# Cached-key attention block: the value loads move from SP's DMA queue to GpSimd's

## The chip, the cores and the metric

The kernel runs on one core of a Trainium2 chip. The metric is the device time of one execution in microseconds; a shorter time is better. The median of three runs is compared.

## What is computed

For a batch of 8, 112 query rows and a model width of 640, there are 32 heads of width 192 and a cache of 512 keys and values per batch and head. All inputs are bf16.

```python
q = (x @ wq).reshape(8, 112, 32, 192).transpose(0, 2, 1, 3)
scores = einsum("bhqd,bhkd->bhqk", q, k_cache) * 192 ** -0.5
p = softmax(scores, axis=-1)
o = einsum("bhqk,bhkd->bhqd", p, v_cache)
out = o.transpose(0, 2, 1, 3).reshape(8, 112, 32 * 192) @ wo
```

The keys and the values are 50 MB each and are read once. The weights `wq` and `wo` are 7.9 MB each.

## The kernel before

Work is cut into **pairs** of heads. The 32 heads form four stages (`hg`, 0 to 3) of eight heads; within a stage the loop runs over the eight batches, and within a batch over four pairs (`lp`), so there are 128 pairs, numbered `ip`. Two pairs that follow each other share one **group** `g` (64 groups): one load of keys and one load of values covers four heads.

All engines follow the same list of periods. In period `i` TensorE (PE) executes, in this order: the scores S of pair `i` (L166 to L169, which read the key tile), half of the transposes of the softmax weights of pair `i-1` (L182), the product with the values PV of pair `i-2` (L200, L206), the other half of the transposes, the output projection O of pair `i-3` (L234, L235), and the query projection Q of pair `i+2` (L262). ScalarE (ACT) does the exponentials and part of the PSUM evictions, VectorE (DVE) the row maxima, scalings and the rest. The order is written out by hand in `DEFAULT_ORDERS`, and semaphores join the engines: `sS` counts scores done, `sPV` counts value products done, `mK[j]`, `mV[j]`, `mWQ`, `mWO` and `mXN` are raised by 16 when a load has landed.

**Keys.** SP issues one transposing DMA for each group (`issue_k`, L477) into one of six buffers `kt[g % 6]`, after the scores of group `g-6` are done. The source is cut into rows of 256 bytes, 3,072 of them in a load of 768 KB.

**Values.** SP issues one plain DMA for each group (`issue_v`, L489), directly after the group's keys, into one of six buffers `vt[g % 6]`, after the value products of group `g-6` are done. A load is 128 partitions by 4 heads by 768 elements: 512 rows of 1,536 bytes, 768 KB. The last two value buffers hold `x` at the start, so value loads 4 and 5 also wait until PE has transposed `x` (`sXT`).

SP's list is thus K0, V0, K1, V1 and so on, with three waits at the start: K1 waits for weight block 1 of stage 0, K2 for block 3, K3 for the last part of `x`.

**Weights.** GpSimd (POOL) issues them, with `x`, in a list ordered by period (`dmas`, filled by `add`). Stage 0 is loaded at the start: four blocks of `wq` (L578, 480 KB) and four of `wo` (L599, L603, L605), the latter after the landing of certain keys. The weights of stages 1 to 3 are cut into 20 pieces of `wq` (L581, 96 KB) and 16 of `wo` (L601 to L607), and spread over the stage before. Each of these pieces waits in `k_landed_wait` until the keys and the values of a certain group have landed:

```python
gK = min(NGRP - 1, max(0, (period + cfg.get("KOFF", 2)) // 2))
W(gp, mK[gK % NKB], 16 * (gK // NKB + 1))
gV = min(NGRP - 1, max(0, (period + cfg.get("VOFF", 0)) // 2))
if period >= 2:
    W(gp, mV[gV % NVB], 16 * (gV // NVB + 1))
```

GpSimd executes its list in order, so what stands behind a wait waits too.

At the start PE transposes batch 0 of `x` (L402), projects pairs 0 and 1 with weight blocks 0 and 1, computes the scores of pair 0, projects pair 2 with block 2, transposes the other seven batches of `x`, and goes on with period 1.

Of the kernel before, what the change touches and what calls it, by code (L numbers as in the profile page):

```python
# [20 lines left out]
def build_mha_kernel(nc, x, k_cache, v_cache, wq, wo, out, cfg=None):  # L21
    cfg = dict(cfg or {})
# [12 lines left out]
    G = 4  # L35
# [8 lines left out]
    def heads_of(ip):  # L44
        u, hg, b, lp = unit_of(ip)
        h0 = hg * HG + 2 * lp
        return b, h0
# [22 lines left out]
    with ExitStack() as es:  # L70
# [55 lines left out]
        def wsem(lst, hg, lp):  # L126
            return lst[(hg % 2) * PPU + lp]
# [18 lines left out]
        def W(eng, s, v):  # L146
            if v > 0:
                eng.wait_ge(s, v)
# [312 lines left out]
        @block.sync  # L461
        def _(sp):
            if not XPE:
                sp.dma_start_transpose(xT_sb[:, :, :], x.rearrange("b s d -> (b s) d")).then_inc(mX, 16)
            EARLY_LEAD = cfg.get("EARLY_LEAD", 0)
            EARLY_N = cfg.get("EARLY_N", 12)

            def issue_k(g):
                b, h0 = heads_of(2 * g)
                kb = g % NKB  # L470
                if g >= NKB:
                    W(sp, sS, 4 * (g - NKB) + 4)
                if EARLY_LEAD and g < EARLY_N and g >= EARLY_LEAD:
                    W(sp, sS, 4 * (g - EARLY_LEAD) + 4)
                src = k_cache[b, h0:h0 + G].rearrange("u (r q) d -> (u r) (q d)", q=4)
                dst = kt[kb][:].rearrange("p a m c -> p (a m) c")
                sp.dma_start_transpose(dst, src).then_inc(mK[kb], 16)  # L477

            def issue_v(g):
                b, h0 = heads_of(2 * g)  # L480
                vb = g % NVB
                if g >= NVB:
                    W(sp, sPV, 2 * (g - NVB) + 2)
                if EARLY_LEAD and g < EARLY_N and g >= EARLY_LEAD + 1:
                    W(sp, sPV, 2 * (g - EARLY_LEAD - 1) + 2)
                if XPE and g in (NVB - 2, NVB - 1):
                    W(sp, sXT, B)
                src = v_cache[b, h0:h0 + G].rearrange("u (r q) d -> r u (q d)", q=4)
                sp.dma_start(vt[vb][:, :, :], src).then_inc(mV[vb], 16)  # L489

            STARTUP = cfg.get("STARTUP", False) and PPU == 4 and NGRP > 5
            if STARTUP:
                issue_k(0)
                issue_k(1)
                issue_v(0)
                W(sp, wsem(mWQ, 0, 3), 16)
                issue_k(2)
                issue_v(1)
                W(sp, wsem(mWO, 0, 1), 48)
                issue_k(3)  # L500
                issue_v(2)
                W(sp, wsem(mWO, 0, 3), 48)
                issue_k(4)
                issue_v(3)
                issue_v(4)
                for g in range(5, NGRP):
                    issue_k(g)
                    issue_v(g)
            else:
                VLAG = cfg.get("VLAG", 0)  # L510
                SPGATE = cfg.get("SPGATE", True) and XPE and PPU >= 4
                for g in range(NGRP + VLAG):
                    if g < NGRP:
                        G1 = cfg.get("SPG1", 1)
                        if SPGATE and g == G1:
                            W(sp, wsem(mWQ, 0, 1), 16)
                        if SPGATE and g == G1 + 1:
                            W(sp, wsem(mWQ, 0, 3), 16)
                        if SPGATE and g == G1 + 2 and B > 4:
                            W(sp, mXN[2], 16)  # L520
                        issue_k(g)
                    if 0 <= g - VLAG < NGRP:
                        issue_v(g - VLAG)
            for b in range(B):
                u = (NHG - 1) * B + b
                if OUTT:
                    W(sp, aOF, b + 1)
                else:
                    W(sp, dOA, u + 1)
                sp.dma_start(out[b], o_out[:, b, :]).then_inc(mOUT[b % 2], 16)  # L530
            for ob in range(2):
                nb = len([b for b in range(B) if b % 2 == ob])
                if nb:
                    sp.wait_ge(mOUT[ob], 16 * nb)

        @block.gpsimd
        def _(gp):
# [11 lines left out]
            def add(need, fn):  # L549
                dmas.setdefault(need, []).append(fn)  # L550
# [4 lines left out]
            def k_landed_wait(period):  # L555
                gK = min(NGRP - 1, max(0, (period + cfg.get("KOFF", 2)) // 2))
                W(gp, mK[gK % NKB], 16 * (gK // NKB + 1))
                gV = min(NGRP - 1, max(0, (period + cfg.get("VOFF", 0)) // 2))
                if period >= 2:
                    W(gp, mV[gV % NVB], 16 * (gV // NVB + 1))  # L560

            STARTUP = cfg.get("STARTUP", False) and PPU == 4 and NGRP > 5

# [20 lines left out]
            def wo_dma(hg, lp, piece, period):  # L584
                wb = hg % 2
                if hg >= 2:
                    W(gp, sO, (hg - 1) * B * PPU)
                if hg == 0 and XPE:
                    if piece == 0:
                        gK = min(NGRP - 1, max(0, period // 2 + cfg.get("WOG", -2)))  # L590
                        W(gp, mK[gK % NKB], 16 * (gK // NKB + 1))
                elif period >= 0 and (hg == 0 or cfg.get("PACE_ALL", True)):
                    k_landed_wait(period)
                r0 = hg * WQC + lp * 2 * DH
                rows = wo[r0:r0 + 2 * DH, :].rearrange("(two r) d -> r two d", two=2, r=DH)
                dstv = wo_sb[:, wb, 3 * lp:3 * lp + 3, :]
                sm = wsem(mWO, hg, lp)
                if piece == 0 and hg == 0:
                    gp.dma_start(dstv[:, 0:3:2, :], rows[0:128, :, :]).then_inc(sm, 16)  # L599
                elif piece == 0:  # L600
                    gp.dma_start(dstv[:, 0, :], rows[0:128, 0, :]).then_inc(sm, 16)  # L601
                elif piece == 1:
                    gp.dma_start(dstv[0:64, 1, :], rows[128:192, 0, :]).then_inc(sm, 16)  # L603
                elif piece == 2:
                    gp.dma_start(dstv[64:128, 1, :], rows[128:192, 1, :]).then_inc(sm, 16)  # L605
                else:
                    gp.dma_start(dstv[:, 2, :], rows[0:128, 1, :]).then_inc(sm, 16)  # L607

            for hg in range(NHG):
                items = []  # L610
                for lp in range(PPU):
                    if wq_npieces(hg) == 1:
                        items.append((first_pair(hg, lp) - 2, 0, lp, "wq", None))
                    else:
                        for dcp in range(DC):
                            items.append((first_pair(hg, lp) - 2, 0, lp, "wq", dcp))
                    for piece in range(wo_npieces(hg)):
                        items.append((first_pair(hg, lp) + 3, 1, lp, "wo", piece))
                items.sort()
                for j, (need, _, lp, kind, piece) in enumerate(items):  # L620
                    if hg == 0:
                        period = need
                    else:
                        start = first_pair(hg - 1, 0) + cfg.get("W_START", 8)
                        span = B * PPU - cfg.get("W_START", 8) - 6
                        period = start + (j * span) // len(items)
                    if kind == "wq":
                        add(period, lambda hg=hg, lp=lp, period=period, piece=piece: wq_dma(hg, lp, period, piece))
                    else:
                        add(period, lambda hg=hg, lp=lp, piece=piece, period=period: wo_dma(hg, lp, piece, period))  # L630
            if XPE and B > 1:
                def fx():
                    n1 = min(B, 4)
                    gp.dma_start(vt[NVB - 2][0:SQ, :, :].rearrange("p u c -> p (u c)")[:, D:n1 * D].rearrange("p (b d) -> p b d", d=D),
                                 x[1:n1].rearrange("b s d -> s b d")).then_inc(mXN[1], 16)
                    if B > 4:
                        gp.dma_start(vt[NVB - 1][0:SQ, :, :].rearrange("p u c -> p (u c)")[:, 0:(B - 4) * D].rearrange("p (b d) -> p b d", d=D),
                                     x[4:B].rearrange("b s d -> s b d")).then_inc(mXN[2], 16)
                dmas.setdefault(-1, []).append(fx)
# [62 lines left out]
```

## Time and profile before

| What | Value |
|---|---|
| Median of 3 runs | 501.38 us |
| Lowest and highest run | 500.34 and 502.07 us |
| Span of the profiled execution | 499.2 us |
| Median of the runs less this span | 2.2 us |
| PE busy in the span | 479.0 us (96%) |
| VectorE busy | 446.6 us (89%) |
| ScalarE busy | 355.1 us (71%) |
| GpSimd busy | 71.5 us (14%) |
| Moved by DMA | 119.90 MB, mean 240 GB/s |
| Key loads (SP, 64), issue to landing | median 9.9 us |
| Value loads (SP, 64), issue to landing | median 5.8 us |

The page has no time of the profiled execution beside its span, which runs from its first to its last instruction; the runs are timed around the whole execution. A difference that is worked out in the span is therefore carried over to the median. In the lists of DMA queues, q1 is what SP issues and q0 is what GpSimd issues; a share counts the time of the packets against 16 engines, and as packets of one engine overlap it can be over 100%.

### The profile page before, as it was taken

How to read it: one execution, taken by the hardware profiler on the slowest of the kernel's cores; microseconds unless marked ns; L12 is line 12 of the kernel's file. 1: busy time of each engine (PE TensorE's matmuls, PEld its weight loads, DVE VectorE, ACT ScalarE, POOL GpSimd, SP SyncE). 2: the span in 40 equal slices, each digit the busy share in tenths (PEclk: the TensorE clock that was granted, in tenths of full speed). 3: DMA queues.
4: the chain of work that ended last, by engine and by line, in shares of the span. 5: the costliest groups of instructions: out<-in, count | busy, mean ns of one | idle time of the engine just before them, and what ended most of it. 6: DMA issues, size and time to landing. Idle time of an engine off the chain costs nothing.

```text
span 499.2 us, 18678 instructions
## 1 busy us (share of the span) xinstructions
PE 479.0 (96%) x6824; PEld 418.9 (84%) x6824; DVE 446.6 (89%) x1610; ACT 355.1 (71%) x898; POOL 71.5 (14%) x133
## 2 busy tenths in 40 slices
PE   1799999999999999999999999999999999999995
PEld 1788888888888888888888888888888888888884
DVE  2589999998999999999999999999999999999994
ACT  1277777777777777777777777777777777777773
POOL 7110133131000133131000122322000000000000
PEclk9999999999999999999999999999999999999999
DMA  9999999999999999999999999999999999999000
GB/s 227 305 285 239 244 256 274 249 265 292 237 249 263 281 261 259 245 265 251 239 247 236 259 290 279 240 282 260 233 272 254 255 260 255 238 258 261 3 14 25
DMA packets 239738, 119.90 MB, mean 240 GB/s; under 512 B 201840, under 2 KB 236480, under 8 KB 239648
## 3 DMA queue, kind: packets, MB, share of 16 engines
q1 hardware_dynamic: 233472, 101.82, 94.4%
q0 software_dynamic: 6176, 16.88, 11.3%
q8 instruction: 56, 0.92, 0.8%
q14 instruction: 34, 0.28, 0.2%
HBM read 67.21 MB, written 1.15 MB: 137 GB/s over the span
## 4 chain that ended last, share of the span: by engine, by line
PE 93%; DMA 2%; issue 1%; DVE 1%; POOL 1%; ACT 0%; DVEq 0%; POOLq 0%; ACTq 0%
PE ps L262 19%; PE ps L234 16%; PE ps L182 13%; PE ps L200 10%; PE ps L206 8%; PE ps L166 6%; PE ps L169 6%; PE ps L167 6%; PE ps L168 6%; PE ps L235 4%; DMA wq_sb<-in_wq_dram 2%; DVE xT_sb L409 1%; POOL wq_sb L578 0%; DVE s_sb L332 0%; DVE o_out L377 0%
## 5 line engine op out<-in xcount | busy, mean ns | idle before, releaser
L284 ACT ACTIVATE p_sb<-s_sb,nmx 112x512 bf16<-112x512 f32 x256 | 181.6, 712 | 3.1 <-DVE s_sb L332 2.1
L332 DVE TENSOR_SCALAR_CACHE_REDUCE s_sb<-ps 112x512 f32<-112x512 f32 x256 | 166.3, 686 | 16.2 <-PE ps L169 14.0
L278 ACT ACTIVATE pT_sb<-ps 128x448 bf16<-128x448 f32 x128 | 69.5, 543 | 88.4 <-PE ps L182 88.4
L262 PE MATMUL ps<-xT_sb,wq_sb 128*128 128x112 bf16 x1920 | 118.0, 215 | 5.2 <-DMA wq_sb<-in_wq_dram 5.2
L234 PE MATMUL ps<-wo_sb,oT_sb 128*112 128x512 bf16 x384 | 118.3, 380 | 0.0
L262 PEld LDWEIGHTS ps<-xT_sb,wq_sb 128*128 128x128 bf16 x1920 | 103.8, 99 | 16.7 <-DMA wq_sb<-in_wq_dram 4.4
L182 PE MATMUL ps<-dg,p_sb 112*128 112x112 bf16 x1024 | 94.0, 214 | 1.8 <-ACT p_sb L284 1.6
L272 ACT ACTIVATE qs<-ps 128x336 bf16<-128x336 f32 x128 | 57.6, 450 | 45.0 <-PE ps L262 41.8
L338 DVE CAST pT_sb<-ps 128x448 bf16<-128x448 f32 x128 | 79.9, 624 | 5.3 <-PE ps L182 1.4
L235 PE MATMUL ps<-wo_sb,oT_sb 128*112 128x128 bf16 x384 | 83.9, 219 | 0.0
L182 PEld LDWEIGHTS ps<-dg,p_sb 112*128 112x128 bf16 x1024 | 64.5, 98 | 14.4 <-ACT p_sb L284 1.9
L166 PE MATMUL ps<-kt,qs 128*112 128x256 bf16 x256 | 70.8, 277 | 2.5 <-issue 1.9
L200 PE MATMUL ps<-pT_sb,vt 128*128 128x112 bf16 x1024 | 71.8, 213 | 0.1
L167 PE MATMUL ps<-kt,qs 128*112 128x256 bf16 x256 | 70.4, 275 | 0.0
L169 PE MATMUL ps<-kt,qs 128*112 128x256 bf16 x256 | 70.4, 275 | 0.0
L168 PE MATMUL ps<-kt,qs 128*112 128x256 bf16 x256 | 70.3, 275 | 0.0
L234 PEld LDWEIGHTS ps<-wo_sb,oT_sb 128*112 128x112 bf16 x384 | 49.7, 129 | 22.3
L581 POOL DMA_DIRECT2D wq_sb<-in_wq_dram x60 | 32.1, 539 | 188.5 <-DMA kt<-in_k_cache_dram 182.4
L308 DVE TENSOR_SCALAR dg<-ident,rinv 112x112 bf16<-112x112 bf16 x256 | 52.9, 249 | 5.0 <-issue 0.5
L200 PEld LDWEIGHTS ps<-pT_sb,vt 128*128 128x128 bf16 x1024 | 56.5, 98 | 0.9 <-issue 0.5
L291 ACT ACTIVATE oT_sb<-ps 128x336 bf16<-128x336 f32 x128 | 55.3, 432 | 1.7 <-PE ps L206 1.7
L235 PEld LDWEIGHTS ps<-wo_sb,oT_sb 128*112 128x112 bf16 x384 | 50.0, 130 | 0.0
(38 smaller groups left out, 498.5 us busy)
## 6 DMA issues: line engine op xcount, KB each, us to landing
vt<-in_v_cache_dram SPq DMA_DIRECT2D x64, 768.0 KB, 5.8
wq_sb<-in_wq_dram POOLq DMA_DIRECT2D x60, 96.0 KB, 5.3
wo_sb<-in_wo_dram POOLq DMA_DIRECT2D x24, 160.0 KB, 5.6
wo_sb<-in_wo_dram POOLq DMA_DIRECT2D x32, 80.0 KB, 5.1
wq_sb<-in_wq_dram POOLq DMA_DIRECT2D x4, 480.0 KB, 10.2
wo_sb<-in_wo_dram POOLq DMA_DIRECT2D x4, 320.0 KB, 10.9
out_dram<-o_out SPq DMA_DIRECT2D x8, 140.0 KB, 4.4
kt<-in_k_cache_dram SPq DMA_TRANSPOSE x64, 9.9
```

The costliest lines, as they stand in the source:

```text
L166: pe.matmul(bk[:, 0:256], qs[:, qb, EA[h], :], ktb[:, :, 0, cs], start=True, stop=False)
L167: pe.matmul(bk[:, 0:256], qs[:, qb, ET[h], :], ktb[:, :, 1, cs], start=False, stop=True)
L168: pe.matmul(bk[:, 256:512], qs[:, qb, OC[h], :], ktb[:, :, 2, cs], start=True, stop=False)
L169: pe.matmul(bk[:, 256:512], qs[:, qb, OH[h], :], ktb[:, :, 1, cs], start=False, stop=True).then_inc(sS, 1)
L182: mm = pe.matmul(ps[:, 2 + h, j * SQ:(j + 1) * SQ], p_sb[:, pslot, j * 128:(j + 1) * 128], dg[:, dslot, :], start=True, stop=True)
L200: pe.matmul(ps[:, 4, oc * SQ:(oc + 1) * SQ], vtb[:, u, q * 192: q * 192 + 128], pT_sb[:, ptb, h, j * SQ:(j + 1) * SQ], start=(j == 0), sto ...
L234: pe.matmul(ps[0:SQ, 6, :], oT_sb[:, ob, c, :], wo_sb[:, wb, 3 * lp + c, 0:512], start=first, stop=last)
L235: mm = pe.matmul(ps[0:SQ, 7, 0:128], oT_sb[:, ob, c, :], wo_sb[:, wb, 3 * lp + c, 512:640], start=first, stop=last)
L262: mm = pe.matmul(ps[:, 5, c * SQ:(c + 1) * SQ], lhsT, xT_sb[:, dc, b * SQ:(b + 1) * SQ], start=(dc == 0), stop=(dc == DC - 1))
L284: act.activation(p_sb[:, Hh % NP, :], s_sb[:, Hh % NSS, :], ACTF.Exp, bias=nmx[:, Hh % NS:Hh % NS + 1], scale=-1.0, accum_out=rsum[:, Hh % ...
L332: dve.tensor_scalar(s_sb[:, Hh % NSS, :], ps[0:SQ, h, :], -scale, None, op0=ALU.mult, op1=ALU.min, accum_out=nmx[:, Hh % NS:Hh % NS + 1]). ...
L338: dve.tensor_copy(pT_sb[:, ip % NPT, 1, :], ps[:, 3, 0:4 * SQ]).then_inc(dPTE, 1)
```

## The change

SP issues the keys alone, with its three waits at the start as before. The 64 value loads go into GpSimd's list. V0 stands at the head of period 0, behind `x` and weight blocks 0 and 1 and ahead of blocks 2 and 3. V1 to V5 stand in periods 5, 7, 7, 8 and 8, and each waits until the keys of its own group have landed. From group 6 on V(g) stands in period `2g - 3` and waits for the value products of group `g-6`, as it did on SP. Weight pieces wait for keys only, no longer for values. The programs of PE, VectorE and ScalarE are the same. Options of SP's list that are off by default fall away.

```diff
@@ sync
-            def issue_v(g):
-                ...
-                if g >= NVB:
-                    W(sp, sPV, 2 * (g - NVB) + 2)
-                ...
-                if XPE and g in (NVB - 2, NVB - 1):
-                    W(sp, sXT, B)
-                src = v_cache[b, h0:h0 + G].rearrange("u (r q) d -> r u (q d)", q=4)
-                sp.dma_start(vt[vb][:, :, :], src).then_inc(mV[vb], 16)
...
-                    if 0 <= g - VLAG < NGRP:
-                        issue_v(g - VLAG)
+            SPGATE = XPE and PPU >= 4
+            for g in range(NGRP):
+                if SPGATE and g == 1:
+                    W(sp, wsem(mWQ, 0, 1), 16)
+                if SPGATE and g == 2:
+                    W(sp, wsem(mWQ, 0, 3), 16)
+                if SPGATE and g == 3 and B > 4:
+                    W(sp, mXN[2], 16)
+                issue_k(g)
@@ gpsimd
                 W(gp, mK[gK % NKB], 16 * (gK // NKB + 1))
-                gV = min(NGRP - 1, max(0, (period + cfg.get("VOFF", 0)) // 2))
-                if period >= 2:
-                    W(gp, mV[gV % NVB], 16 * (gV // NVB + 1))
...
+            def issue_v(g):
+                b, h0 = heads_of(2 * g)
+                vb = g % NVB
+                if g >= NVB:
+                    W(gp, sPV, 2 * (g - NVB) + 2)
+                elif g > 0:
+                    W(gp, mK[g], 16)
+                if XPE and g in (NVB - 2, NVB - 1):
+                    W(gp, sXT, B)
+                src = v_cache[b, h0:h0 + G].rearrange("u (r q) d -> r u (q d)", q=4)
+                gp.dma_start(vt[vb][:, :, :], src).then_inc(mV[vb], 16)
+
+            v_early = [0, 5, 7, 7, 8, 8]
+            dmas.setdefault(0, []).insert(0, lambda: issue_v(0))
+            for g in range(1, NGRP):
+                add(v_early[g] if g < NVB else 2 * g - 3, lambda g=g: issue_v(g))
```

More of the change, by code (lines that the diff above doesn't have):

```diff
@@ L477, in issue_k @@
                 sp.dma_start_transpose(dst, src).then_inc(mK[kb], 16)
-            def issue_v(g):
-                b, h0 = heads_of(2 * g)
-                vb = g % NVB
-                if g >= NVB:
-                    W(sp, sPV, 2 * (g - NVB) + 2)
-                if EARLY_LEAD and g < EARLY_N and g >= EARLY_LEAD + 1:
-                    W(sp, sPV, 2 * (g - EARLY_LEAD - 1) + 2)
-                if XPE and g in (NVB - 2, NVB - 1):
-                    W(sp, sXT, B)
-                src = v_cache[b, h0:h0 + G].rearrange("u (r q) d -> r u (q d)", q=4)
[L489 to L521, printed above, removed]
-                    if 0 <= g - VLAG < NGRP:
-                        issue_v(g - VLAG)
+            SPGATE = XPE and PPU >= 4
[7 more added lines that the diff above has]
+                issue_k(g)
             for b in range(B):
```

## The prediction

> **What bounds the kernel now.** I read the page first. PE is busy for 479.0 of 499.2 us, and the DMA engines are busy in every slice up to the 37th.
>
> ```profile
> PE 479.0 (96%) x6824; PEld 418.9 (84%) x6824; DVE 446.6 (89%) x1610; ACT 355.1 (71%) x898; POOL 71.5 (14%) x133
> DMA  9999999999999999999999999999999999999000
> q1 hardware_dynamic: 233472, 101.82, 94.4%
> ```
>
> Both could be the bound, so the next view is what PE waited for (us in total, times, longest).
>
> ```profile
> PE ps L402 <- DMA vt<-in_x_dram: 7.2, 1, 7.2
> PE ps L262 <- DMA wq_sb<-in_wq_dram: 5.2, 3, 1.9
> PE ps L166 <- issue: 1.9, 5, 0.8
> ```
>
> After the start PE waits only in front of L166, the first score matmul, and that line needs its keys. The timeline of PE places the five waits (the number in brackets); four are shown, the one left out is 0.35 us at 117.03.
>
> ```profile
> 28.15 0.29 PE L166 MATMUL ps<-kt,qs 128*112 128x256 bf16 x1 [0.80 <-issue]
> ...
> 93.99 0.29 PE L166 MATMUL ps<-kt,qs 128*112 128x256 bf16 x1 [0.31 <-issue]
> ...
> 109.22 0.29 PE L166 MATMUL ps<-kt,qs 128*112 128x256 bf16 x1 [0.25 <-issue]
> ...
> 124.68 0.29 PE L166 MATMUL ps<-kt,qs 128*112 128x256 bf16 x1 [0.18 <-issue]
> ```
>
> So there are 0.80 us at the start and 0.31 + 0.25 + 0.35 + 0.18 = 1.09 us between 93 and 125 us, where the first prefetched weights share the DMA engines. Elsewhere PE runs without a gap: in the chain of waits the projection (L262) returns every 3.65 us, 7.29 us for a group of two pairs. The timeline of SP's queue shows why keys are late there (start, duration):
>
> ```profile
> 104.64 6.97 SPq L477 DMA_TRANSPOSE kt<-in_k_cache_dram  x1
> 111.65 0.58 SPq L489 DMA_DIRECT2D vt<-in_v_cache_dram  x1
> 112.28 7.11 SPq L477 DMA_TRANSPOSE kt<-in_k_cache_dram  x1
> 119.43 0.58 SPq L489 DMA_DIRECT2D vt<-in_v_cache_dram  x1
> 120.06 6.96 SPq L477 DMA_TRANSPOSE kt<-in_k_cache_dram  x1
> ```
>
> SP never pauses; the key instruction itself is held back, 7 us here against 3.03 us for the first one into an empty queue. One group takes (120.06 - 104.64) / 2 = 7.71 us, more than PE's 7.29. Without weights (key issues at 133.46 and 164.69, five groups) it takes 6.25 us. The DMA side is therefore late in the first weight stage alone, and gains about 1 us a group elsewhere.
>
> **What the transfers cost.** Keys alone move at 290 GB/s (65.3 to 67.3 us): 786,432 bytes take 2.71 us. GpSimd's queue alone moves 330 GB/s (14.2 to 17.6 us): a value load of the same size would take 2.38 us there, four weight pieces 1.19 us. Together 6.28 us, so 1.4 us of the 7.71 is lost between transfers. How the two queues share the engines is in the DMA answers for three windows, 18:23, 70:74.4 and 74.4:76 (packets, MB, share):
>
> ```profile
> q0 software_dynamic: 414, 1.50, 94.7%
> q1 hardware_dynamic: 407, 0.10, 11.4%
> ```
>
> ```profile
> q1 hardware_dynamic: 2844, 1.00, 123.6%
> ```
>
> ```profile
> q0 software_dynamic: 162, 0.37, 79.7%
> ```
>
> In the first, keys met a backlog of weights: the weights took nearly everything (0.30 MB/us against 0.02), and the sum stayed at the full rate. In the second, four weight pieces issued by GpSimd from 70.04 us moved nothing until the key transfer ended, 4.4 us later; the third shows them moving then. So a value load from GpSimd starts some 3 to 4.5 us after its issue and, once started, is ahead of the keys.
>
> **The change, part by part.** (1) SP loses 64 issues of 0.58 us, 37 us. Nothing comes of the issue time itself: SP's key instruction is held by the DMA engines, not by SP.
>
> (2) GpSimd gains 64 issues. Its rows are 0.74 us (L634) and 0.87 us (L578) for loads of 336 and 640 rows; 512 rows give an estimate of 0.82, so 52 us. It is busy 71.5 of 499 us and waits over 260 us for keys: hidden. Without that cover it would delay `wq` pieces, which stage 1 needs only after 125 us and has had issued by 87 us.
>
> (3) Key loads follow each other directly, and values come by a second queue. A key load no longer has the preceding value load (2.38 us) ahead of it, and PE needs values later than keys: group 1's scores start at 28.15, its values are read at 36.04. The 0.42 us a group that the weight stage falls behind (7.71 - 7.29) ate a lead of under 2 us; 2.4 us more covers the 1.09 us that was waited. Bounds: a gain of 1.09, or nothing; I take 1.09, since the sums above are work that does not depend on the queue.
>
> (4) The start. Load V0 moves from SP into GpSimd's queue, before weight block 2; SP's key load K1 still waits for block 1. Block 1 had V0 beside it (8 to 14 us: 1.19 MB of GpSimd's queue, 0.79 MB of SP's) and will land earlier, so K1 joins about 3 us sooner. Block 2 has the same bytes ahead of it plus what K1 gets in those 3 us: 0.06 MB, 0.2 us. The chain from block 2 (L262 at 17.87) through the transposes of x to the projection that ended at 27.36 so ends at 27.6, and K1, with that much done early, lands no later: of the 0.80 us I take 0.5. Bounds: 0.80 (block 2 not delayed) and -0.1 (block 2 a whole issue of 0.87 later).
>
> (5) New waits. V1 is issued only when K1 has landed, V2 to V5 likewise after theirs, and later ones behind paced weight pieces; behind a waiting value load on GpSimd stand the weights. Critical is V1: the piece that is issued at this point now (L599, 28.34) lands 5.3 us later with 320 KB; 448 KB more add 1.4 us. K1 0.5 us sooner gives 27.8 + 6.7 = 34.5; PE reads V1 at 35.5. Cost 0 with 1 us to spare; the other end is a whole key load (2.7 us) in front, a stall of 1.7 us. V4 stands behind two weight pieces that wait for K5. K1's transfer fills the time to 26.0; then come K2 to K5 (10.8 us), V1 to V3 (7.1) and the last `wo` block (480 KB, 1.5), so K5 lands at about 45.4 + 2 = 47.4, and V4 after a start of up to 4.5, the two pieces (0.6), its own 2.4 and 0.6 to land at 55.5. PE reads it at 57.9: cost 0.
>
> Sum: 1.09 + 0.5 = 1.59 us. From the profiled span that is 499.2 - 1.6 = 497.6; the median of the runs lies 2.2 us above the span, so 501.38 - 1.59 = **499.8 us**. All waits gone would be 1.89, 499.5. The tail (PE's 1.60 us gap at 491, waiting for ACT) is untouched.
>
> [...]
>
> **The rivals.** *No change (B).* The gain is eaten: V1 0.5 to 1.7 us late, or block 2 later. 501.4 within 0.7. For it: the margins of 0.2 and 1 us.
>
> *Values starve behind an unbroken key stream (C), slower.* No key transfer in this trace is followed by another at once, and GpSimd's pieces of 70.04 waited for the end of the one that ran. If the second queue only gets in when SP's is empty, V1 waits behind K2 to K7 (six buffers, two of them freed by then): from 26.0 six times 2.71 = 42.3, plus 2.38 and about 0.6 to land, 45.2; PE needed it at 36.0: 9.2 us, once, 510.6. It decides from the third key load ahead of V1 (37.1, a stall of 1.1 us). Against it: the 18 to 23 us window, and x's first load, which moved 0.13 MB between 4 and 5 us in the middle of K0.
>
> [...]
>
> *Mixing costs bandwidth (D), slower.* Between 2 and 7 us, K0 and x's load together moved 201 GB/s, against 290 for keys alone. If breaking into the keys loses 0.5 us more per group, the nine groups of the first weight stage cost 4.5 us, 505.9; at 201 GB/s throughout, keys and values alone would take 7.8 us a group, 34 us over all. Against it: 18 to 23 us, where the mixed rate was 321.
>
> **How the numbers follow.** The forecast has 0.52, B 0.12, C 0.20, D 0.16. About 0.3%, 1.5 us, is what a measurement of this kernel can tell from no change. The forecast's own range, 499.1 to 500.6, crosses that line: 0.40 of its 0.52 beyond, 0.12 within. Faster 0.40, same 0.24, slower 0.36. The range goes from 499.0 (all 1.89 us and some spread) to 507.0, past D's near price and into C.
>
> **What would show it.** Right: no wait at L166 between 93 and 125 us, S of group 1 near 27.6, V1 landed before PE's first read of it, key issues well ahead after 60 us. Wrong: a PE wait at L200 near 36 us (C), its length telling how many key loads went first; waits at L166 or L200 in every weight stage and DMA rates below 240 GB/s (D); or a later first L262 for block 2 (B).

## The result, and the profile after

The changed kernel takes 633.33 us (median of 4 runs, 626.59 to 637.17) against 500.86 us for the kernel before, run beside it. The ratio is 1.256, with an interval of 1.251 to 1.261: it is 26% slower. The ratio leaves out 637.17 and 636.15, which count as slow runs, being over 1.5% above the fastest; their granted clock was that of the other two (0.911 and 0.905 against 0.913 and 0.915). The forecast was 499.8 us, and 507.0 was the end of its range.

The page after, of an execution of 637.17 us with a span of 635.4:

```profile
PE 506.7 (80%) x6824; PEld 439.0 (69%) x6824; DVE 456.2 (72%) x1610; ACT 354.4 (56%) x898; POOL 119.3 (19%) x197
...
PEclk9699599889959998896796797999898999999999
DMA  9999999999999999999999999999999999999300
...
q1 hardware_dynamic: 199680, 51.49, 66.5%
q0 software_dynamic: 18464, 67.22, 41.9%
```

PE is no longer the bound: it is busy for 80% of the span, where it was 96%. The DMA engines still show work in every slice up to the 37th, though they move the same bytes in 136 us more. The span grew from 499.2 to 635.4 us. Of these 136.2 us, 108.5 are PE standing idle (128.7 against 20.2), and 27.7 are PE being slower (506.7 busy against 479.0), with a granted clock of 0.911 on average against 0.999.

What PE waited for (total, times, longest):

```profile
PE ps L166 <- issue: 59.3, 11, 13.5
PE ps L262 <- issue: 18.3, 5, 6.1
PE ps L200 <- DMA vt<-in_v_cache_dram: 15.8, 1, 15.8
PE ps L168 <- issue: 7.0, 2, 3.5
```

L166 is again the first reader of the keys, with 59.3 us instead of 1.9. Values (L200) are waited for once. So most of it is late keys, and the transfers say why. First the whole first weight stage, 60 to 126 us, before and then after (packets, MB, mean rate):

```profile
DMA packets 31721, 17.52 MB, mean 265 GB/s; under 512 B 26099, under 2 KB 31023, under 8 KB 31708
```

```profile
DMA packets 16093, 11.21 MB, mean 170 GB/s; under 512 B 14207, under 2 KB 14495, under 8 KB 16086
```

The DMA engines had work throughout and moved two thirds of the bytes. Then two stretches of the kernel after in which both queues have work, 17 to 23 us and 61 to 68 us:

```profile
DMA packets 1001, 1.91 MB, mean 319 GB/s; under 512 B 640, under 2 KB 640, under 8 KB 1001
## 3 DMA queue, kind: packets, MB, share of 16 engines
q0 software_dynamic: 505, 1.79, 93.6%
q1 hardware_dynamic: 496, 0.13, 11.2%
```

```profile
DMA packets 660, 1.17 MB, mean 167 GB/s; under 512 B 416, under 2 KB 427, under 8 KB 660
...
q0 software_dynamic: 269, 1.07, 71.8%
q1 hardware_dynamic: 391, 0.10, 31.6%
```

In the first, the two queues move one packet each in turn (505 and 496): a key packet of 256 bytes goes for each large packet, and keys creep at 0.02 MB/us, but the sum is at the full rate. In the second the keys have 0.10 MB in 7 us and the other queue has slowed too, so that the sum is half; the key load issued there took 31.1 us to land (the median was 9.9 before and is 12.0 after: some loads are very late, most are not). This second mode is the loss. It isn't there throughout. From 500 to 560 us, when the last weights have been issued and GpSimd issues values alone, the list by time (PE busy, the other engines, clock, DMA share, GB/s) has

```profile
500.00:560.00 60.00, 59.05 (x848) 51.09 (x846) 56.65 (x200) 44.14 (x112) 6.00 (x8) 1.00 1.18 262
```

and PE loses 1 us of 60.

Some 34 us of PE's waits are another matter. They lie in the middle of a run of matmuls, where the program has no wait: L262 (18.3 us) and L168 (7.0) in the list above, and behind them L200 (3.5), L206, L167 and L235. One of them:

```profile
118.37 0.36 PE L262 MATMUL ps<-xT_sb,wq_sb 128*128 128x112 bf16 x4
124.78 1.18 PE L262 MATMUL ps<-xT_sb,wq_sb 128*128 128x112 bf16 x11 [6.05 <-issue]
```

The projection had done 4 of its 15 matmuls and went on 6 us later. From 122 to 124 us the DMA list has

```profile
q8 instruction: 1, 0.02, 3.5%
```

This is a fetch of instructions (16 KB), which ended at 123.4, 1.4 us before PE went on. All eleven such stops end 1.2 to 1.7 us after the end of one of the trace's 56 fetches of this size. Whose instructions a fetch brings is not in the trace; that PE waited for its own is a guess, and no run tests it.

The start came at the time that was forecast. The first scores of group 1:

```profile
27.43 0.29 PE L166 MATMUL ps<-kt,qs 128*112 128x256 bf16 x1 [0.81 <-issue]
```

GpSimd's first two value loads after V0:

```profile
27.62 0.78 POOL L602 DMA_DIRECT2D vt<-in_v_cache_dram  x1 [13.58 <-DMA kt<-in_k_cache_dram]
...
30.18 0.78 POOL L602 DMA_DIRECT2D vt<-in_v_cache_dram  x1
```

S of group 1 began at 27.43 (27.6 forecast), and V1, issued at 27.62, landed 5.5 us later at 33.2 (34.5 forecast), while SP had issued keys without a pause since 10.28.

### The profile page after: what moved, and what is told of

It is laid out like the page before. It is cut to its first block, busy times and chain, and to the rows that moved or that the text cites. A ratio compares the mean times of both kernels' runs of the same rounds, so it can differ in the third digit from the quotient of the medians.

```text
span 635.4 us, 18644 instructions
## 1 busy us (share of the span) xinstructions
PE 506.7 (80%) x6824; PEld 439.0 (69%) x6824; DVE 456.2 (72%) x1610; ACT 354.4 (56%) x898; POOL 119.3 (19%) x197
## 4 chain that ended last, share of the span: by engine, by line
PE 72%; issue 15%; DMA 6%; SPq 5%; DVE 1%; POOL 0%; ACT 0%; DVEq 0%; POOLq 0%; ACTq 0%
PE ps L262 14%; PE ps L234 13%; PE ps L182 10%; PE ps L200 8%; PE ps L206 6%; SPq L477 5%; PE ps L166 5%; PE ps L168 4%; PE ps L167 4%; PE ps L169 4%; PE ps L235 3%; DMA vt<-in_v_cache_dram 3%; DMA kt<-in_k_cache_dram 2%; DMA wq_sb<-in_wq_dram 1%; DVE s_sb L332 0%
## 5 line engine op out<-in xcount | busy, mean ns | idle before, releaser
L262 PE MATMUL ps<-xT_sb,wq_sb 128*128 128x112 bf16 x1920 | 121.8, 218 | 23.9 <-issue 18.3
L262 PEld LDWEIGHTS ps<-xT_sb,wq_sb 128*128 128x128 bf16 x1920 | 106.7, 101 | 36.3 <-issue 19.8
L234 PE MATMUL ps<-wo_sb,oT_sb 128*112 128x512 bf16 x384 | 121.9, 389 | 0.2 <-issue 0.2
L166 PE MATMUL ps<-kt,qs 128*112 128x256 bf16 x256 | 73.8, 288 | 59.8 <-issue 59.3
L182 PE MATMUL ps<-dg,p_sb 112*128 112x112 bf16 x1024 | 97.1, 219 | 2.2 <-ACT p_sb L284 1.6
L200 PE MATMUL ps<-pT_sb,vt 128*128 128x112 bf16 x1024 | 76.4, 221 | 19.8 <-DMA vt<-in_v_cache_dram 15.8
L602 POOL DMA_DIRECT2D vt<-in_v_cache_dram x64 | 48.3, 755 | 228.2 <-PE ps L206 199.8
L235 PE MATMUL ps<-wo_sb,oT_sb 128*112 128x128 bf16 x384 | 85.2, 222 | 0.8 <-issue 0.8
L168 PE MATMUL ps<-kt,qs 128*112 128x256 bf16 x256 | 73.4, 287 | 7.0 <-issue 7.0
L200 PEld LDWEIGHTS ps<-pT_sb,vt 128*128 128x128 bf16 x1024 | 60.6, 102 | 20.8 <-issue 20.5
L167 PE MATMUL ps<-kt,qs 128*112 128x256 bf16 x256 | 73.4, 287 | 1.6 <-issue 1.6
L169 PE MATMUL ps<-kt,qs 128*112 128x256 bf16 x256 | 73.3, 286 | 0.0
L166 PEld LDWEIGHTS ps<-kt,qs 128*112 128x112 bf16 x256 | 35.0, 137 | 54.6 <-issue 53.8
L291 ACT ACTIVATE oT_sb<-ps 128x336 bf16<-128x336 f32 x128 | 55.5, 433 | 21.3 <-PE ps L206 21.3
L234 PEld LDWEIGHTS ps<-wo_sb,oT_sb 128*112 128x112 bf16 x384 | 50.9, 133 | 23.4 <-issue 1.9
```

The source lines that it names most:

```text
L166: pe.matmul(bk[:, 0:256], qs[:, qb, EA[h], :], ktb[:, :, 0, cs], start=True, stop=False)
L167: pe.matmul(bk[:, 0:256], qs[:, qb, ET[h], :], ktb[:, :, 1, cs], start=False, stop=True)
L168: pe.matmul(bk[:, 256:512], qs[:, qb, OC[h], :], ktb[:, :, 2, cs], start=True, stop=False)
L169: pe.matmul(bk[:, 256:512], qs[:, qb, OH[h], :], ktb[:, :, 1, cs], start=False, stop=True).then_inc(sS, 1)
L182: mm = pe.matmul(ps[:, 2 + h, j * SQ:(j + 1) * SQ], p_sb[:, pslot, j * 128:(j + 1) * 128], dg[:, dslot, :], start=True, stop=True)
L200: pe.matmul(ps[:, 4, oc * SQ:(oc + 1) * SQ], vtb[:, u, q * 192: q * 192 + 128], pT_sb[:, ptb, h, j * SQ:(j + 1) * SQ], start=(j == 0), sto ...
```

## The experiments

Theory 1: a transposing load works only while the 16 DMA engines keep step, and packets of a second queue break that. Theory 2: GpSimd's queue is too slow for the values. Theory 3: the waits and the order on GpSimd's list hold the loads up. The kernel before took 500 to 501.4 us (median) beside every run.

**e1: the changed kernel with key loads that don't transpose.**

```diff
-                sp.dma_start_transpose(dst, src).then_inc(mK[kb], 16)
+                src = k_cache[b, h0:h0 + G].rearrange("u k d -> (u k d)").rearrange("(x p c) -> p x c", p=128, c=128)
+                dst = kt[kb][:].rearrange("p a m (x c) -> p (a m x) c", c=128)
+                sp.dma_start(dst, src).then_inc(mK[kb], 16)
```

> The changed kernel with its 64 key loads made plain: the same 768 KB in the same 3,072 rows of 256 bytes on SP's queue, not transposed (so the keys in the tile are not the right ones). Values stay on GpSimd. Theory 1, that a transposing load needs all engines in step and the packets of a second queue break the step: without the transposition the loss goes, 500 to 515 us, and the DMA rate between 60 and 70 us goes from about 100 to over 220 GB/s. Theory 2, that GpSimd's queue is itself too slow for the values: still over 600 us. Theory 3, that the new waits and the order of GpSimd's list make the values late: still over 600 us, as these waits stay.

Measured: 506.69 us, ratio 1.012 (1.007 to 1.017). All waits, lists and rows are those of the change; only the transposition is gone, and with it 127 of the 132 us. (The rate from 60 to 70 us was 203 GB/s in the kernel after, not about 100 as the expectation has it; the slow stretch is 61 to 68 us.) The same 61 to 68 us of this run:

```profile
DMA packets 1423, 2.42 MB, mean 346 GB/s; under 512 B 866, under 2 KB 962, under 8 KB 1421
...
q0 software_dynamic: 685, 2.21, 91.8%
q1 hardware_dynamic: 736, 0.18, 12.4%
```

The queues take turns here too, at 346 GB/s instead of 167. Theory 3 falls: its waits are all here.

**e2: the same edit in the kernel before**, as a control.

> The kernel before with the same plain key loads (the keys in the tile are not the right ones): the control for the run above. If plain rows of 256 bytes move as fast as transposed ones, 497 to 502 us by all theories; if it is much slower than 502, the run above has to be read against this one and not against the kernel before.

Measured: 500.80 us, ratio 0.9995 (0.997 to 1.002). With the values on SP behind their keys it made no difference whether the keys transpose, so e1's gain is not that plain loads are cheaper.

**e3: values on ScalarE's hardware queue instead of GpSimd's**, with V(g) in period 2g - 7 of ACT's list from V8 on, and earlier ones in periods 0 to 8.

```diff
-                gp.dma_start(vt[vb][:, :, :], src).then_inc(mV[vb], 16)
+                act.dma_start(vt[vb][:, :, :], src).then_inc(mV[vb], 16)
```

> The changed kernel with its 64 value loads issued by ScalarE's queue, not GpSimd's, at points where the value products waited for are done. Theory 1: any second queue with standing work beside the transposes breaks their step, over 560 us, PE waiting for keys (L166) by tens of us. Theory 2 (GpSimd's queue is slow): 498 to 515 us. Theory 3 (waits and order on GpSimd): 498 to 520 us, as the values no longer stand behind weight pieces.

Measured: 623.32 us, ratio 1.245 (1.236 to 1.254). Theory 2 falls: ACT's queue does it as well. Two stretches of this run, 69 to 72 and 73 to 76 us (q10 is ACT's queue, q8 fetches instructions):

```profile
DMA packets 1284, 1.13 MB, mean 376 GB/s; under 512 B 657, under 2 KB 1284, under 8 KB 1284
...
q10 hardware_dynamic: 643, 0.96, 86.1%
q1 hardware_dynamic: 641, 0.16, 24.1%
```

```profile
DMA packets 468, 0.38 MB, mean 127 GB/s; under 512 B 272, under 2 KB 467, under 8 KB 467
...
q10 hardware_dynamic: 211, 0.30, 65.9%
q1 hardware_dynamic: 256, 0.07, 40.8%
q8 instruction: 1, 0.02, 2.2%
```

While the queues take turns (643 and 641 packets) the rate is full. A microsecond later it is a third. It broke off at 72.9 and again at 74.4 us, each time about half a microsecond after an instruction fetch began (a short one at 72.33, the one listed at 73.77); between the two stops it was full.

**e9: e3 with the values cut into rows of 256 bytes, like the keys** (the values in the tile are then not in their places).

```diff
+                src = v_cache[b, h0:h0 + G].rearrange("u k d -> (u k d)").rearrange("(x p c) -> p x c", p=128, c=128)
```

> Values on ScalarE's queue as in the run before it, but each load in 3,072 rows of 256 bytes, the size of the key rows, and not in 512 rows of 1,536 (the values in the tile are then not the right ones). Theory 1a: each step of a transposing load waits for about one packet of the other queue on some engine, so the loss follows the packet size: 500 to 540 us. Theory 1b: engines get out of step and stay so whatever the packet size: 580 to 640 us.

Measured: 614.88 us, ratio 1.228 (1.223 to 1.233), in the range of theory 1b. The time by itself decides nothing, since ACT's own work now waits behind its issues of 3,072 rows (one took 8.96 us) and PE waits 53.9 us for ACT. The rate says more: from 126 to 500 us this run moved 200 GB/s, the kernel after 188, the kernel before 232, all with busy DMA engines. Equal packets don't mend it.

**e4: half of the values back on SP** (even groups from SP after their keys, odd ones from GpSimd).

> The changed kernel with the even groups' values back on SP behind their keys; the odd groups' stay on GpSimd. Theory 1 (mixing): SP's stream is broken by a value load in every second group and half the bytes mix, so about half of the loss, 540 to 590 us. Theory 3 (waits and order on GpSimd's list): about half as well, if the lateness comes from single loads, or 500 to 520 if it comes from the length of the backlog on GpSimd.

Measured: 543.87 us (two runs, 531.6 and 556.15): for half of the values, a quarter to two fifths of the loss.

**e5: keys one at a time.** SP issues K(g) only when K(g-1) has landed, so that values could come in between.

```diff
+                if g > 0:
+                    W(sp, mK[(g - 1) % NKB], 16 * ((g - 1) // NKB + 1))
                 issue_k(g)
```

> The changed kernel with one more wait: SP issues a key load only when the key load before it has landed, so that its queue runs dry between two of them for some 3 us, about what a value load of 768 KB needs by itself. Theory 1: the values move in these gaps, the mixing and most of the loss go, 500 to 540 us. Theory 2 and theory 3: a wait more and nothing made faster, 630 us or more.

Measured: 627.23 us (two runs, 614.70 and 639.77), far outside what theory 1 had forecast. The edit didn't separate the two: the landing of K(g-1) releases the next key load and GpSimd's list at the same moment, and the value's packets begin some 3 us later, inside the key load. One key load of this run was issued at 109.3 us, and from 115.7 to 118.9 us the queues carried

```profile
q0 software_dynamic: 267, 0.90, 80.8%
...
q1 hardware_dynamic: 32, 0.00, 0.8%
```

It was reported landed after 9.7 us, at 119.0, when the other queue's values had ended. The 32 packets of SP's queue are not its rows, as 32 rows of 256 bytes would be 0.01 MB: the load landed about 3 us after its last row. In the kernel before, the 64 key loads landed 0.5 to 3.7 us after their last row, 2.0 at the median, so these 3 us don't show a delay by the other queue.

**e12: values and keys really apart** (each value load waits for its own keys to land, K(g) waits for V(g-2) to land).

```diff
+                if g > 1:
+                    W(sp, mV[(g - 2) % NVB], 16 * ((g - 2) // NVB + 1))
                 issue_k(g)
...
-                elif g > 0:
-                    W(gp, mK[g], 16)
+                if g > 0:
+                    W(gp, mK[g % NKB], 16 * (g // NKB + 1))
```

> The changed kernel with two more waits that keep the values on GpSimd but mostly apart from the keys: every value load waits for its own group's keys to land, and SP issues the keys of group g only when the values of group g-2 have landed. Theory 1: about 6.6 us a group without weights and 7.8 with four pieces of them, so 505 to 540 us, although it waits more. Theories 2 and 3 (GpSimd's queue too slow, waits and order): 630 us or more.

Measured: 578.48 us (two runs, 565.86 and 591.10), more than theory 1 had forecast. Some of it still mixed (172 GB/s from 116 to 128 us). Where nothing mixed, the handing over cost instead: GpSimd's value issues, one for each group, came 7.6, 7.8 and 8.1 us apart between 142 and 166 us, over PE's 7.29. Two queues that take turns by semaphores are no cure here.

**e6: the order of the change without its second queue.** In the kernel before, SP issues V(g) after K(g+1).

```diff
-                VLAG = cfg.get("VLAG", 0)
+                VLAG = cfg.get("VLAG", 1)
```

> The kernel before with the values one group later on SP's queue: keys of group g+1 are issued ahead of the values of group g, all still on SP. If the 1.09 us that PE waited between 93 and 125 us were a matter of order in one queue, as the prediction held, they go: 499.5 to 500.2 us, and no wait at the first score matmul in that stretch. If values come too late instead, or the order does not matter, 500.9 or more.

Measured: 528.68 us, ratio 1.055 (1.051 to 1.059), in the range given for late values or no effect, but for another reason. The weight pieces on GpSimd wait for keys and for values, and now the values come last, so the pieces are released while a key load runs. GpSimd's waits, and the DMA engines from 94.7 to 101.7 us:

```profile
POOL wq_sb L581 <- DMA vt<-in_v_cache_dram: 145.1, 12, 52.2
```

```profile
DMA packets 3258, 1.18 MB, mean 169 GB/s; under 512 B 3122, under 2 KB 3204, under 8 KB 3257
...
q1 hardware_dynamic: 3111, 0.84, 96.5%
q0 software_dynamic: 146, 0.32, 27.9%
```

It is the same rate with other data: 0.32 MB of weights inside a key load, 169 GB/s. In the kernel before, the landing of a key load released the pieces, and their packets came as the next key load ended.

**e11: e6, and the pieces wait for keys alone.**

```diff
-                gV = min(NGRP - 1, max(0, (period + cfg.get("VOFF", 0)) // 2))
-                if period >= 2:
-                    W(gp, mV[gV % NVB], 16 * (gV // NVB + 1))
```

> The run with values one group later on SP, with one more edit: weight pieces wait for keys alone, as before a key landing lets them go, not a value landing. Theory 1 says that the lag itself cost little and that the 27 us came from weight pieces that now arrived while a key load ran; with the key landing as the signal they arrive again as a key load ends: 499.5 to 504 us. If the values were simply late through the lag, this edit changes nothing: 525 to 530 us.

Measured: 498.83 us, ratio 0.9956 (0.9935 to 0.9976): 0.4% faster than the kernel before. Only the moment at which the pieces start differs from e6. From 60 to 126 us (time, PE busy, the other engines, clock, DMA share, GB/s):

```profile
60.00:126.00 66.00, 66.00 (x960) 57.74 (x957) 62.43 (x227) 49.80 (x128) 15.47 (x29) 1.00 1.18 270
```

and PE's waits at L166:

```profile
PE ps L166 <- issue: 4.2, 1, 4.2
```

PE has no idle time in the first weight stage. Its one wait at L166 is at the start (25.93 us), where it grew from 0.80 us to 4.2. So keys ahead of values is a gain, as step (3) had it, on one queue. (Whether the gate without the order would do is not tested.)

**e8 and e10: the weights of stages 1 to 3 on SP as well**, after a value load each, so that nothing mixes; e10 adds VLAG = 1.

> The kernel before with the 108 weight pieces of stages 1 to 3 issued by SP, each behind the values of the group that it waited for, so that after the start the chip has one queue alone. If a second queue beside the transposes costs DMA time even in the kernel before (1.4 us a group were lost in the weight stage, with 1.19 us of weights in it), the key loads come every 7.3 us or less there and the waits between 93 and 125 us go: 499.5 to 500.3 us. If the loss is that of changing from one transfer to another, the weight stage stays near 7.7 us a group, 500.5 to 502.

> The kernel before with one queue alone after the start (weight pieces of stages 1 to 3 on SP) and the values one group later, so that order is changed and nothing can mix. The prediction's step that a key load without its predecessor's values ahead of it ends the waits for keys: 499.5 to 501 us and under 1 us of waits at the first score matmul. If order is not what these waits hang on: 503 to 505 us, as without the lag.

Measured: e8 503.86 us, ratio 1.005 (1.002 to 1.007), and e10 501.58, ratio 0.999 (0.997 to 1.002). Both lie outside their forecasts. Four weight issues take 2.29 us of SP per group, and in e8 the groups then came 8.5 to 8.9 us apart between 94 and 120 us. One queue for all is no gain either.

**e13 to e16: how little mixing is enough.** GpSimd issues 192 side loads of 8 KB, two per pair from pair 20 to 115, into a buffer that nobody reads, in the kernel before (e13) and in e2 (e14).

```diff
+                gp.dma_start(side[j:j + 1, :], wq[n:n + 1, 0:4096]).then_inc(mSD[j], 16)
```

> The kernel before, with 192 side loads: from pair 20 to pair 115 GpSimd issues two loads per pair of one 8 KB row each, paced by PE's scores, into a buffer that nobody reads. They are 1.57 MB, 1.3% of all that is moved: about 5 us at the 290 GB/s that keys alone have, spread over 48 groups, each of which had about 1 us to spare outside the weight stages. [...] Theory 1 (a transposing load goes on only when all 16 engines do): each side load that meets a key load stops the whole load for about 0.5 us; key loads run most of the time, so 48 groups lose 1 to 2 us each against about 1 us to spare: 520 to 575 us, with waits of PE at L166. Rival (the price comes from many packets of two queues taking turns, not from one engine being late): nearly no packets are mixed, 500 to 505 us.

> The same 192 side loads of one 8 KB row, in the kernel before with its key loads not transposed (the keys in the tile are then not the transposed ones). Theory 1: the other 15 engines go on, so 500 to 505 us, like the same kernel without side loads (500.8). If this is slow as well, the side loads cost by themselves (GpSimd's list held up, one engine overloaded) and the run before it shows nothing about transposition.

Measured: e13 518.48 us, ratio 1.034 (1.030 to 1.039); e14 501.88, ratio 1.002 (1.000 to 1.004). No run shows the 0.5 us for which a side load of e13 was to stop a key load: GpSimd's queue has 6,144 packets more than before, 32 for each side load, half of them of 512 bytes, so that a side load went in 16 pieces and not as one row. e15 and e16 repeat the pair with 4,093 elements.

> The run with 8 KB side loads showed 32 packets for each of them: they were spread over all 16 engines in pieces of 512 bytes, and no engine was late by itself. Here a side load is one row of 4,093 elements, a prime number, so that it can't be cut evenly: 8,186 bytes in one piece on one engine. At 18 GB/s (a sixteenth of the 290 GB/s of keys alone) that holds one engine for some 0.45 us. In-step theory: each side load that meets a key load stops all of it for about 0.45 us; 192 of them, four in five meeting keys, are 70 us, of which some 40 us are spare: 515 to 560 us, not less than with the spread loads (518). Taking-turns theory (what costs is that packets of two queues alternate on every engine): a sixteenth of the mixed packets, so 500 to 506 us.

> The same one-engine side loads with key loads that are not transposed (the keys in the tile are then not the transposed ones). In-step theory: the other 15 engines go on, 500 to 505 us. Slower than that would mean that a late engine costs any load, transposing or not.

Measured: e15 518.80 us, ratio 1.031 (1.025 to 1.037); e16 502.22, ratio 1.004 (1.002 to 1.005). Again there are 32 packets for each side load, but now one of them holds the whole row. From 400 to 440 us, where no weights move, the kernel before, then e15, then e16:

```profile
q1 hardware_dynamic: 22202, 10.07, 111.8%
```

```profile
DMA packets 21733, 9.22 MB, mean 231 GB/s; under 512 B 18873, under 2 KB 21703, under 8 KB 21725
...
q1 hardware_dynamic: 21021, 8.94, 114.0%
q0 software_dynamic: 704, 0.18, 2.3%
```

```profile
q1 hardware_dynamic: 22342, 10.09, 108.8%
q0 software_dynamic: 702, 0.18, 2.3%
```

704 packets are 22 side loads. 21725 - 21703 = 22 packets have between 2 and 8 KB: the rows of 8,186 bytes, each a single packet. They are all of the 0.18 MB; the other 31 packets of a side load have 4 bytes each. So each side load of e15 had one packet with nearly all of its bytes, and both forecasts of the in-step theory came: 515 to 560 us for e15 and 500 to 505 for e16. Taking turns had 500 to 506 for e15. A count of packets would be the same for e13 and e15, so the times alone don't part it from one engine held by a row. The trace does. Two side loads in the middle of a key load, 150 to 152 us of e15 (GB/s in 40 slices of 50 ns), and two beside plain keys, 175 to 177 us of e16:

```profile
GB/s 297 282 297 282 292 297 282 307 282 461 261 276 266 271 266 276 256 26 20 51 317 225 271 271 118 0 15 15 20 26 225 251 282 287 287 292 282 292 287 292
...
q0 software_dynamic: 4, 0.02, 2.0%
```

```profile
GB/s 323 277 323 272 328 312 497 225 328 282 302 210 272 338 292 251 440 246 266 200 241 261 302 169 271 261 256 241 261 241 225 276 230 261 215 246 251 246 210 246
```

In e15 the two rows start at 150.50 and 151.00 and hold one engine for 0.31 us each (2.0% of 16 engines' 2 us). The key load stops at 150.85 for 0.15 us and at 151.20 for 0.3 us, at 0 to 51 GB/s after the first slice; one idle engine of 16 would leave some 270 of the 290 (an estimate). Over the whole trace, 29 of the 34 rows that met a key load at its full rate were followed within 1 us by a slice of 0.1 us below 60 GB/s, against 16 of 410 other moments of such loads with no other queue's packet near, and none of 23 beside the plain keys of e16.

As a price, SP's queue moved 10.07 - 8.94 = 1.13 MB less in the 40 us, which is 4.5 us at its 0.252 MB/us: by this one stretch about 0.20 us for a side load whose 8 KB would take 0.03 us at 290 GB/s. Beside plain keys nothing was lost (10.09 MB).

The same came after instruction fetches. In the kernel before, from 193 to 195 us:

```profile
GB/s 625 256 297 246 292 266 276 271 266 282 210 15 0 0 0 0 0 0 0 0 0 5 10 10 5 10 5 10 10 10 10 5 15 5 10 10 10 10 26 251
...
q8 instruction: 1, 0.02, 3.2%
```

In e2, keys plain, from 191 to 193 us:

```profile
GB/s 317 353 287 609 302 307 317 230 328 312 271 236 317 287 271 246 236 266 287 246 246 210 276 266 230 225 225 276 236 266 210 236 256 220 256 241 246 241 246 246
...
q8 instruction: 1, 0.02, 3.5%
```

The first fetch began at 193.05 and held one engine for 1.0 us (3.2% of 16 engines' 2 us). The transposing load went on for half a microsecond and then stood at 0 to 26 GB/s for 1.4 us, from 193.55 to 194.95, most of that time after the fetch had ended. Nine more fetches of this trace are followed in the same way by a stop of 1.2 to 1.45 us. The second fetch began at 191.19, and the plain load beside it never fell below 210. So theory 1 stands this far: where a packet of another queue held one engine for 0.31 or 1.0 us, a transposing load mostly stopped soon after, and a plain one did not. That it stops because the engines lose step is a reading that no run shows. Stops came without such a packet too: in the kernel before, the rate was 0 to 46 GB/s for 1.2 us from 183.05 us, and from 182 to 184 us only SP's queue moved packets. What started those is not shown.

## Why the prediction was wrong

**The step that failed** is (3), in the words "since the sums above are work that does not depend on the queue". The work of a transposing load does depend on it: from 60 to 126 us the DMA engines, busy as before, moved 11.21 MB in place of 17.52, and instead of a gain of 1.09 us came a loss of 132. The order in that step was right: e11, which has the order and not the second queue, lost no time between 60 and 126 us and came out 1.8 us faster.

**The mechanism that decided was in the prediction, as rival D, with its price mis-sized.** It was given 4.5 us, and 34 at most; it is 132 us. Three things went into that:

- The mixed rate was taken from 18 to 23 us (321 GB/s), and the 2 to 7 us window with 201 GB/s was set aside. But in the first, keys moved 0.10 MB in 5 us: it shows weights at full speed while the keys stood almost still, and prices no keys. The second had a whole key load in it and was the nearer row; the slow mixed stretches ran at 167 GB/s after the change, 169 in e6 and 172 in e12.
- The upper price counted keys and values alone, 7.8 us against PE's 7.29 for each group. All 119.9 MB at 201 GB/s are 597 us, some 95 us more than before. At the 189 GB/s measured over the whole span they are 634.
- PE slowed as well: its granted clock was 0.911, and lower where it idled (0.84 from 60 to 126 us with 39.8 of 66 us busy, 1.00 from 500 to 560 with 59.05 of 60), and PE's work took 27.7 us longer. No term had that, nor the 34 us of stops in the middle of a run of matmuls.

**Why before showed no price.** Its mixed stretches were few because each weight piece was released by a landing, and moved only when the next key load had ended (the 70 to 74.4 us window). The prediction read this as "a value load from GpSimd starts some 3 to 4.5 us after its issue and, once started, is ahead of the keys". e6 shows what it hid: the same pieces, released by values instead, cost 27 us.

**Point by point.** (1) and (2): GpSimd's issue took 755 ns (0.82 forecast), its busy time was 119.3 us (71.5 + 52 = 123.5 forecast), and that was hidden. (4): 27.43 us against 27.6, by two misses that cancel: the projection ahead of the scores ended at 26.6, not 27.6, and the wait for K1 stayed at 0.81 us, where 0.5 of 0.80 was to go. (5): V1 had time to spare, right. V4 had not: K5 landed at 54.7 (47.4 forecast), V4 was issued at 56.11 and took 20.5 us to land, at 76.6 (55.5 forecast), and PE waited 15.8 us for it at L200. The list had a margin of 2.4 us, and the slow transfers took more. Rival C didn't happen: V1 landed at 33.2 us while SP issued keys without a pause. Rival B is refuted by the size. The sign given to "waits at L166 or L200 in every weight stage and DMA rates below 240 GB/s (D)" is what came.

**What stays open.** Why some mixed stretches keep the full rate and others fall to half: after a packet that held one engine a transposing load stopped for 0.15 us (e15) to 1.4 us (the kernel before), but how such stops add up to a stretch of 7 us at 167 GB/s isn't worked out. How the 132 us divide between the values on GpSimd and the weights, whose waits the change altered too, isn't separated either: weights alone cost 27 us in e6, and values alone cost next to nothing from 500 to 560 us, but from 330 to 376 us, where no weights were issued, PE was busy for only 27.5 of 46 us.

## What to carry to other kernels

Keep a transposing DMA stream on one queue with the other large loads that run at the same time, and order them there (in this kernel 498.83 us against 633.33); if small loads must come from another queue, release them so that they move between two transposing loads (498.83 us in e11 against 528.68 in e6). When a trace gives a total rate for two queues, look at what each one moved before taking it as the price of mixing: a full sum can hide a stream that stands still (319 GB/s from 17 to 23 us, with 0.13 MB of keys in it). A rival's price is worked out over all bytes that would go at the bad rate, and over what else slows with it.

## What the runs showed of the hardware

- Transposing loads beside a second queue: 167 GB/s (61 to 68 us after the change), 169 (e6) and 172 (e12) in mixed stretches, against 346 with plain rows (e1, 61 to 68 us). The kernel was slow with GpSimd's queue (633.33 us) and with ACT's (623.32). It wasn't so throughout: 262 GB/s after the change from 500 to 560 us.
- Little was enough: 192 side loads with 1.3% more bytes cost 3.4% and 3.1% beside transposing keys (e13, e15), 0.2% and 0.4% beside plain ones (e14, e16).
- A transposing load stopped after a packet of another queue had held one engine: for 0.15 and 0.3 us with packets of 8,186 bytes (0.31 us each, e15), for 1.4 us with an instruction fetch (1.0 us, the kernel before). A plain load beside such a fetch never fell below 210 GB/s (e2, 191 to 193 us).
- After the change PE stopped eleven times in the middle of a run of matmuls, for 34 us in all, and went on 1.2 to 1.7 us after the end of an instruction fetch each time.
- Key loads were reported landed 0.5 to 3.7 us after their last row in the kernel before, 2.0 at the median; one in e5, with the other queue's values at the same time, about 3 us.
- PE's granted clock was lower where PE idled much: 0.84 from 60 to 126 us after the change with 39.8 of 66 us busy, against 1.00 in the same stretch of e11, busy throughout.
